# Planning GpSimd's instructions behind VectorE's shift passes, with a newly picked program order

## The chip, the core and the metric

The kernel runs on one core of a Trainium2 chip. The core's engines each execute their own instruction stream in order and meet only through semaphores: TensorE (PE; its weight loads are PEld), ScalarE (ACT), VectorE (DVE), GpSimd (POOL), and SyncE (SP), which here issues the DMAs. The metric is the device time of one execution in microseconds, lower is better. Time before: 1489.41 us, median of three runs (1488.92 to 1489.61).

## What is computed

Two rounds of attention block and feed-forward block on 2048 rows of width 512, with 32 heads of 16 columns:

```python
    x = A_x
    x = x + _A_ref(_layernorm(x, axis=-1), A_wqkv, A_wo)
    x = x + _B_ref(_layernorm(x, axis=-1), B_w1, B_b1, B_w2, B_b2)
    x = x + _A_ref(_layernorm(x, axis=-1), A_wqkv, A_wo)
    x = x + _B_ref(_layernorm(x, axis=-1), B_w1, B_b1, B_w2, B_b2)
    return x
```

`_A_ref` projects to q, k and v, computes `softmax(q k^T / 4) v` per head, and multiplies by `wo`. `_B_ref` is `gelu(x w1 + b1) w2 + b2` with 1792 hidden columns. Nearly all the work around the change is the exponential of the scores: 2 layers x 32 heads x 2048 x 2048 values.

## The kernel before, in words

**Cells.** The scores are cut into cells, each a PSUM bank of 128 keys by 512 columns (256 queries of two heads, or 512 queries of one, as the padded q tile `qp` has it). A layer has 2048 cells, the kernel 4096. A pass is one group of query columns and heads against all its key tiles. The score matmul of a cell (`score`, L1413) reads the keys and `qp`, which GpSimd makes by masking q (`qpad`, L1361).

**Two ways to the exponential.** ScalarE takes two or three cells in one ACTIVATE (`exps`, L1853) and writes bfloat16 into a `pt` buffer. Cells of five chosen key tiles (`KD`) may take the other way, here called D cells: VectorE evacuates one bank (`dfirst`, L1570) as a scaled and biased 16-bit integer, whose bits are a rough bfloat16 exponential; then three more copies of it, shifted by 32, 64 and 96 in the integer, are made, and TensorE adds the products of all four copies with V and three scaled copies of V (`vcopies`, L1342, on GpSimd). Two D cells share a buffer, a pair. For a pair (`dchain`) the first shift is made by GpSimd (L1687, 1024 columns); then VectorE makes both others in one instruction (L1692, 2048 columns), or GpSimd makes one of them (L1700) and VectorE the other (L1698, 1024 columns). L1692 and L1698 are "the shift passes of VectorE". In the program's names the pair buffers are `du`, and parts of `kt` and `v` that are free at the time serve as more of them.

**Who takes a cell.** A group of scores is issued for two or three banks. `swap` may turn the last cell of a group of three into a D cell when, in the planner's clocks, VectorE is free within SWAP us of the group's start; `attach` and `solo` can add D cells in other banks. So the share of the D cells is not fixed; it follows from how busy the planner believes VectorE to be.

**The order is written out by hand-made planning.** When the program is built, `_Sched` plays all work as threads against one clock per engine. `run` (L450) takes from each engine its best instruction that could go (those ready by the engine's clock by priority, else the one ready first), and of these commits the one with the earliest start, over and over. `_ready` (L379) gives the time at which an instruction could go; `_cost` its planned duration; `end` when its result is seen. What goes to the chip is only the order of each engine's instructions and the semaphore waits that data dependencies need. Planned times do not go to the chip.

**The shared port in the plan.** `_Op.port` marks VectorE's shift passes (and its writes of `OTT` and `NMR`). In the plan they never run at the same time as a GpSimd instruction. A marked instruction that would start while a committed GpSimd instruction runs is given that one's end, less HEAD (0.14 us), as ready time (`pool_ops`). A GpSimd instruction that would start while a committed marked one runs is moved behind it (`port_ops`): with a real semaphore wait (`op.lock`) if it would start within CLOSE (0.35 us) of the other's start, else only in the plan:

```python
            for a, b, ev in self.port_ops[-4:]:
                if a <= at < min(a + CLOSE, b - HEAD):
                    at = t = b + LATENCY["dve"]
                    op.lock = ev
                elif a <= at < b - HEAD:
                    at = t = b - HEAD
```

**Pieces.** The 4096 cells are cut into equal pieces of the program; `turn` sets the planner's constants for each piece to one of the ROWS (PIECES says which).

Of the kernel before, what the change touches and what calls it, by code (L numbers as in the profile page):

```python
# [34 lines left out]
DU = 10  # L35
LNP = 7
SWAP = 0.5
ALONE = 3.5
# [11 lines left out]
TAIL = 10  # L50
OPENING = 18
ROUNDS = 2
PTLOW = 5
TOL = 0.2
# [3 lines left out]
QUEUE = 4  # L58
LNQ = 3.5
NAMES = ("SWAP", "SLACK", "LATE", "TOL", "BACKLOG", "OPENING", "TAIL", "PVP", "PTURG", "DUURG", "DULOW", "DWIDE", "RWIDE", "PTLOW", "FPRIO", "MID",  # L60
         "EVAC", "ROUNDS", "ALONE", "AHEAD", "PSHIFT", "QUEUE", "SOLO", "BACK", "SIDE", "BOTH", "DMAX", "PMORE", "DUMORE",)
ROWS = (
# [239 lines left out]
class _Sched:  # L302
# [32 lines left out]
    def _advance(self, th):  # L335
        moved = False
        while th.op is None and not th.done:
# [37 lines left out]
            elif item[0] == "spawn":  # L375
                self.spawn(item[1], item[2])
        return moved

    def _ready(self, op):  # L379
        t = 0.0  # L380
        for k in op.reads:
# [1647 lines left out]
```

## Time and profile before

| | |
|---|---|
| median of the runs | 1489.41 us |
| the profiled execution | 1490.43 us, of which span 1488.6 us |
| ACT busy | 1457.6 us, 98% of the span |
| PE busy | 1432.6 us, 96% |
| DVE busy | 1353.7 us, 91% |
| POOL busy | 942.6 us, 63% |
| granted TensorE clock | 1.0 |

The span is from the first to the last instruction. "Busy" is the time in which an engine has an instruction running; an instruction that waits for something within the engine, after its semaphores, counts as busy for as long as it stands there. DVE's and ACT's neighbouring instructions overlap by some 0.08 us, so that counts times mean durations come out above the busy time.

### The profile page before, as it was taken

How to read it: one execution, taken by the hardware profiler on the slowest of the kernel's cores; microseconds unless marked ns; L12 is line 12 of the kernel's file. 1: busy time of each engine (PE TensorE's matmuls, PEld its weight loads, DVE VectorE, ACT ScalarE, POOL GpSimd, SP SyncE). 2: the span in 40 equal slices, each digit the busy share in tenths (PEclk: the TensorE clock that was granted, in tenths of full speed). 3: DMA queues.
4: the chain of work that ended last, by engine and by line, in shares of the span. 5: the costliest groups of instructions: out<-in, count | busy, mean ns of one | idle time of the engine just before them, and what ended most of it. 6: DMA issues, size and time to landing. Idle time of an engine off the chain costs nothing.

```text
span 1488.6 us, 46274 instructions
## 1 busy us (share of the span) xinstructions
PE 1432.6 (96%) x20012; PEld 436.7 (29%) x20012; DVE 1353.7 (91%) x2332; ACT 1457.6 (98%) x1387; POOL 942.6 (63%) x1032
## 2 busy tenths in 40 slices
PE   8999999999999999999999999999999999999999
PEld 2222222222222222222222222222222222334345
DVE  6589999999998999989879899999989999999994
ACT  7999999999999999999999999999999999999996
POOL 4347657676665776757556575667667667766751
PEclk9999999999999999999999999999999999999999
DMA  6100001153121430214421431001143104411021
GB/s 171 30 2 2 1 15 31 40 157 91 37 44 58 143 87 27 55 38 132 117 65 44 144 107 37 23 2 37 37 129 100 51 23 129 143 25 44 17 66 38
DMA packets 135798, 94.47 MB, mean 63 GB/s; under 512 B 36525, under 2 KB 134574, under 8 KB 135598
## 3 DMA queue, kind: packets, MB, share of 16 engines
q1 hardware_dynamic: 135598, 91.52, 22.1%
q8 instruction: 160, 2.62, 0.7%
q14 instruction: 40, 0.33, 0.1%
HBM read 79.70 MB, written 4.19 MB: 56 GB/s over the span
## 4 chain that ended last, share of the span: by engine, by line
ACT 49%; PE 37%; DVE 12%; POOL 1%; DMA 1%; issue 1%; SPq 0%
ACT pt L1853 42%; PE ps L653 12%; PE ps L1413 12%; PE ps L1917 12%; DVE du L1570 5%; ACT g L1128 3%; DVE du L1692 2%; DVE kt L1570 1%; ACT kt L1853 1%; ACT q L1853 1%; ACT L1128 1%; PE ps L1401 1%; DVE x L1167 1%; ACT L1853 1%; DVE g L1107 0%
## 5 line engine op out<-in xcount | busy, mean ns | idle before, releaser
L1853 ACT ACTIVATE pt<-ps 128x1024 bf16<-128x1024 f32 (+1 forms) x1253 | 1306.9, 1177 | 8.0 <-PE ps L1413 6.1
L1570 DVE TENSOR_SCALAR du<-ps 128x512 uint16<-128x512 f32 x853 | 564.9, 680 | 40.3 <-PE ps L1413 35.8
L1687 POOL TENSOR_SCALAR du<-du 128x1024 uint16<-128x1024 uint16 (+1 forms) x429 | 445.8, 1044 | 232.4 <-DVE du L1570 97.4
L1413 PE MATMUL ps<-qp,kt 32*128 32x512 bf16 x4096 | 548.4, 384 | 25.2 <-ACT pt L1853 13.6
L1917 PE MATMUL ps<-pt,v 128*17 128x512 bf16 (+1 forms) x3159 | 388.2, 359 | 3.4 <-ACT pt L1853 1.1
L1917 PE MATMUL ps<-du,vc 128*17 128x512 bf16 (+1 forms) x2874 | 346.9, 357 | 3.6 <-POOL v L1700 0.8
L1413 PEld LDWEIGHTS ps<-qp,kt 32*128 32x128 bf16 x4096 | 139.5, 91 | 576.5 <-ACT pt L1853 200.5
L1692 DVE TENSOR_SCALAR du<-du 128x2048 uint16<-128x2048 uint16 x336 | 245.4, 744 | 4.2 <-POOL du L1687 4.2
L1917 PE MATMUL ps<-du,v 128*17 128x512 bf16 (+1 forms) x958 | 158.6, 359 | 4.9 <-DVE xt L932 1.6
L1925 PE MATMUL ps<-b2row,zero 128*17 128x512 bf16 x788 | 145.5, 381 | 0.0
L653 PE MATMUL ps<-xf,wr 128*32 128x512 bf16 (+1 forms) x1888 | 128.5, 364 | 1.4 <-DVE g L1107 1.1
L1917 PEld LDWEIGHTS ps<-pt,v 128*17 128x17 bf16 x3159 | 95.6, 88 | 103.8 <-issue 70.4
L1361 POOL TENSOR_SCALAR qp<-q,mask 128x512 bf16<-128x512 bf16 (+1 forms) x91 | 61.4, 675 | 94.3 <-PE ps L1413 42.0
L1570 DVE TENSOR_SCALAR kt<-ps 128x512 uint16<-128x512 f32 x165 | 109.9, 681 | 10.5 <-PE ps L1413 9.7
L1917 PEld LDWEIGHTS ps<-du,vc 128*17 128x17 bf16 x2874 | 96.3, 89 | 76.2 <-issue 42.8
L1687 POOL TENSOR_SCALAR kt<-kt 128x1024 uint16<-128x1024 uint16 x83 | 86.9, 1048 | 49.3 <-DVE du L1692 23.1
L653 PE MATMUL ps<-wr,g 128*32 128x512 bf16 x1408 | 105.0, 383 | 1.1 <-DMA wr<-in_B_w_dram 0.5
L1342 POOL TENSOR_SCALAR vc<-v 128x680 bf16<-128x680 bf16 (+2 forms) x126 | 87.4, 693 | 25.4 <-DVE du L1692 8.2
L1700 POOL TENSOR_SCALAR du<-du 128x1024 uint16<-128x1024 uint16 (+1 forms) x93 | 97.1, 1044 | 8.4 <-DVE du L1692 4.4
L1917 PE MATMUL ps<-kt,vc 128*17 128x512 bf16 (+1 forms) x615 | 96.0, 339 | 1.2 <-DVE kt L1692 0.8
L1107 DVE TENSOR_SCALAR g<-ps,hb1t 128x512 bf16<-128x512 f32 (+1 forms) x112 | 79.0, 706 | 3.9 <-PE ps L653 3.6
L786 POOL TENSOR_SCALAR xln<-x,rstd,nmr 128x512 bf16<-128x512 bf16 x58 | 47.0, 818 | 21.9 <-DVE du L1692 10.9
(110 smaller groups left out, 1451.8 us busy)
## 6 DMA issues: line engine op xcount, KB each, us to landing
wr<-in_B_w_dram SPq DMA_DIRECT2D x228, 256.0 KB, 2.9
wr<-in_A_wqkv_dram SPq DMA_DIRECT2D x24, 256.0 KB, 2.9
x<-in_A_x_dram SPq DMA_DIRECT2D x7, 512.0 KB, 4.1
wr<-in_A_wo_dram SPq DMA_DIRECT2D x10, 256.0 KB, 3.3
kept<-x SPq DMA_DIRECT2D x4, 512.0 KB, 3.5
x<-kept SPq DMA_DIRECT2D x4, 512.0 KB, 3.9
out_dram<-x SPq DMA_DIRECT2D x16, 128.0 KB, 2.2
g<-in_A_wqkv_dram SPq DMA_DIRECT2D x3, 512.0 KB, 5.5
```

Of the source, the lines that this page charges most:

```text
L653: return [lambda e, a=a: e.matmul(out[32 * a:32 * a + 32, :], lhsT=lhsT[:, 32 * a:32 * a + 32], rhs=rhs, start=start, stop=stop, tile_posi ...
L1107: yield _Op("dve", 0.21 + n / 966, lambda e, fc=fc, pb=pb: e.tensor_scalar(T["G"][:, fc, q], pb, T["HB1T"][:, fc:fc + 1], None, op0=ALU.ad ...
L1342: yield _Op("pool", 0.15 + 0.133 * len(js), lambda e, i=i, w=w, v=v, js=js, src=src: e.tensor_scalar(T["VC"][:, v % 2, i, js[0]:js[-1] + 1 ...
L1361: yield _Op("pool", 0.27 + 0.42 * w / 512, lambda e, s=s, q=q, i=i, t=t, w=w: e.tensor_scalar(T["QP"][:, s, w * i:w * i + w], q, T["MASK"] ...
L1413: return (lambda e: e.matmul(o, lhsT=lhsT, rhs=rhs, start=True, stop=True, tile_position=(32 * a, 0)), ["K%d.%d.%d" % (l, gb, kt // 4), "Q ...
L1570: yield _Op("dve", 0.682, lambda e: e.tensor_scalar(u, self.bank(b), E_SCALE, E_BIAS, op0=ALU.mult, op1=ALU.add), reads=["B.%d" % b], writ ...
L1687: one = _Op("pool", 0.15 + 0.45 * n, lambda e, a=a, b=b: e.tensor_scalar(b, a, float(SHIFT), 1.0, op0=ALU.add, op1=ALU.mult), reads=key[0] ...
L1692: two = _Op("dve", 0.152 + 0.266 * n, lambda e: e.tensor_scalar(U[:, 2:4, 0:n, :], U[:, 0:2, 0:n, :], 2 * SHIFT, None, op0=ALU.add), reads ...
L1700: more = _Op("pool", 0.15 + 0.45 * n, lambda e, a=a, c=c: e.tensor_scalar(c, a, float(2 * SHIFT), 1.0, op0=ALU.add, op1=ALU.mult), reads=k ...
L1853: yield _Op("act", 0.065 + 0.4267 * n, lambda e, src=src, dst=dst: e.activation(out=dst, in_=src, func=ACT.Exp, scale=0.25), reads=["B.%d" ...
L1917: op.fns.append(lambda e, o=o, lhsT=q[0][0][m], rhs=q[0][1][:, n * m:n * m + n], a=a, st=st, sp=sp: e.matmul(o, lhsT=lhsT, rhs=rhs, start= ...
L1925: op.fns.append(lambda e, o=self.bank(b)[32 * a:32 * a + 17, :], rhs=rhs, a=a, st=not begun[a], sp=end: e.matmul(o, lhsT=T["ZERO"][:, 0:17 ...
```

## The change

Three things, all in the planner; no instruction's form is altered.

1. In `_ready`, a GpSimd instruction is now held, while a shift pass of VectorE (or another marked VectorE instruction) waits uncommitted whose data are there by GRACE = 1.5 us after the time at which the GpSimd instruction could start. Its ready time becomes that at which the marked one would end, less HEAD, if VectorE did it next. GALL = 1 makes this hold for all of GpSimd's instructions. A new function `bare` gives the data-ready time of the marked one.
2. The rows lose five constants (BACKLOG, OPENING, PTURG, DULOW, EVAC), which keep the values that they have in the module; there are 40 rows instead of 61.
3. PIECES has 80 entries instead of 160, each thus twice as long, with another choice.

```diff
+GRACE = 1.5
+GALL = 1
...
-NAMES = ("SWAP", "SLACK", "LATE", "TOL", "BACKLOG", "OPENING", "TAIL", "PVP", "PTURG", "DUURG", "DULOW", "DWIDE", "RWIDE", "PTLOW", "FPRIO", "MID",
-         "EVAC", "ROUNDS", "ALONE", "AHEAD", "PSHIFT", "QUEUE", "SOLO", "BACK", "SIDE", "BOTH", "DMAX", "PMORE", "DUMORE",)
+NAMES = ("SWAP", "SLACK", "LATE", "TOL", "TAIL", "PVP", "DUURG", "DWIDE", "RWIDE", "PTLOW", "FPRIO", "MID", "ROUNDS", "ALONE", "AHEAD", "PSHIFT",
+         "QUEUE", "SOLO", "BACK", "SIDE", "BOTH", "DMAX", "PMORE", "DUMORE",)
...
-PIECES = (10, 10, 15, 18, 18, 43, 56, 38, 30, 38, 38, 28, 8, 0, 60, 60, 48, 21, 43, 35, 46, 0, 1, 45, 45, 49, 4, 11, 41, 25, 57, 24, 20, 31, 15, 1,
...
+PIECES = (5, 10, 30, 21, 19, 33, 36, 8, 37, 23, 30, 38, 12, 0, 36, 22, 13, 0, 0, 0, 20, 35, 0, 0, 12, 0, 0, 18, 16, 0, 25, 33, 0, 17, 0, 0, 26, 3, 39,
...
+    def bare(self, op):
+        t = 0.0
+        for k in op.reads:
+            if k not in self.P.lastw:
+                return None
+        for ev in self.P.deps(op.reads, op.writes):
+            t = max(t, self.end.get(ev, 0.0) - OWN * (op.eng == "dve" == ev[0]))
+        return t
+
     def _ready(self, op):
...
         if op.eng == "pool":
             at, op.lock = max(t, self.clock["pool"]), None
+            if GRACE and (op.writes[0][:2] == "DU" or GALL):
+                for th in self.threads:
+                    x = th.op
+                    if x is not None and x.port and x.eng == "dve":
+                        y = self.bare(x)
+                        if y is not None and max(y, self.clock["dve"]) <= at + GRACE:
+                            t = max(t, max(y, self.clock["dve"], at) + self._cost(x) - HEAD)
+                at = max(t, self.clock["pool"])
             for a, b, ev in self.port_ops[-4:]:
                 if a <= at < min(a + CLOSE, b - HEAD):
                     at = t = b + LATENCY["dve"]
```

More of the change, by code (lines that the diff above doesn't have):

```diff
@@ L58 @@
 QUEUE = 4
+GRACE = 1.5
+GALL = 1
 LNQ = 3.5
-NAMES = ("SWAP", "SLACK", "LATE", "TOL", "BACKLOG", "OPENING", "TAIL", "PVP", "PTURG", "DUURG", "DULOW", "DWIDE", "RWIDE", "PTLOW", "FPRIO", "MID",
-         "EVAC", "ROUNDS", "ALONE", "AHEAD", "PSHIFT", "QUEUE", "SOLO", "BACK", "SIDE", "BOTH", "DMAX", "PMORE", "DUMORE",)
+NAMES = ("SWAP", "SLACK", "LATE", "TOL", "TAIL", "PVP", "DUURG", "DWIDE", "RWIDE", "PTLOW", "FPRIO", "MID", "ROUNDS", "ALONE", "AHEAD", "PSHIFT",
+         "QUEUE", "SOLO", "BACK", "SIDE", "BOTH", "DMAX", "PMORE", "DUMORE",)
 ROWS = (
[61 rows of a table removed]
-)
-PIECES = (10, 10, 15, 18, 18, 43, 56, 38, 30, 38, 38, 28, 8, 0, 60, 60, 48, 21, 43, 35, 46, 0, 1, 45, 45, 49, 4, 11, 41, 25, 57, 24, 20, 31, 15, 1,
[4 rows of a table removed]
[40 rows of a table added]
+)
+PIECES = (5, 10, 30, 21, 19, 33, 36, 8, 37, 23, 30, 38, 12, 0, 36, 22, 13, 0, 0, 0, 20, 35, 0, 0, 12, 0, 0, 18, 16, 0, 25, 33, 0, 17, 0, 0, 26, 3, 39,
+          4, 0, 3, 1, 19, 21, 13, 23, 0, 31, 28, 10, 7, 11, 6, 27, 2, 30, 34, 0, 15, 0, 27, 36, 32, 31, 29, 10, 33, 0, 16, 17, 14, 38, 24, 9, 19, 0,
+          0, 0, 0)
 CLOSE = 0.35
```

105 rows, old and new, of tables (PIECES, ROWS) are left out of this document.

## The prediction

> **What bounds the kernel now.** I read the page's busy times and chain first, then the middle of the execution as one stretch, then VectorE's shift passes one line at a time, then the waits.
>
> ```profile
> span 1488.6 us, 46274 instructions
> PE 1432.6 (96%) x20012; PEld 436.7 (29%) x20012; DVE 1353.7 (91%) x2332; ACT 1457.6 (98%) x1387; POOL 942.6 (63%) x1032
> ACT 49%; PE 37%; DVE 12%; POOL 1%; DMA 1%; issue 1%; SPq 0%
> ```
>
> The stretch from 50 to 1400 us (columns: length, then busy time and count of PE, PEld, DVE, ACT, POOL):
>
> ```profile
> 50.00:1400.00 1350.00, 1303.75 (x17640) 378.65 (x17640) 1258.15 (x2135) 1342.72 (x1264) 877.67 (x950) 1.00 0.22 61
> ```
>
> ScalarE works 1342.72 of 1350 us: 7.3 us of idle time in all. So in the middle the time is the work that ScalarE is given, and it changes only if (a) ScalarE gets other work, or (b) others keep it waiting. VectorE idles 91.9 us there, GpSimd 472. The groups of ScalarE's exponentials price (a):
>
> ```profile
> L1853 ACT ACTIVATE pt<-ps 128x1024 bf16<-128x1024 f32 x922 | 887.5, 1062 | 6.5 <-PE ps L1413 5.1
> L1853 ACT ACTIVATE pt<-ps 128x1536 bf16<-128x1536 f32 x330 | 472.7, 1499 | 1.4 <-PE ps L1413 1.0
> ```
>
> A group of three that loses a cell to VectorE costs 1499 - 1062 = 437 ns less. The price of a D cell, by VectorE's lines (min/median/max of one in ns) and groups:
>
> ```profile
> L1692 DVE TENSOR_SCALAR du<-du x336: 416/684/1668, 70.0 to 1459.6; 128x2048 uint16<-128x2048 uint16 x166, 128x1024 uint16<-128x1024 uint16 x2
> L1698 DVE TENSOR_SCALAR du<-du x93: 282/419/1304, 117.0 to 1461.1; 128x1024 uint16<-128x1024 uint16 x92, 128x512 uint16<-128x512 uint16 x1
> L1570 DVE TENSOR_SCALAR du<-ps 128x512 uint16<-128x512 f32 x853 | 564.9, 680 | 40.3 <-PE ps L1413 35.8
> L1692 DVE TENSOR_SCALAR du<-du 128x2048 uint16<-128x2048 uint16 x332 | 243.6, 748 | 4.2 <-POOL du L1687 4.2
> L1692 DVE TENSOR_SCALAR kt<-kt 128x2048 uint16<-128x2048 uint16 x58 | 41.0, 707 | 0.0
> L1692 DVE TENSOR_SCALAR v<-v 128x2048 uint16<-128x2048 uint16 x32 | 24.6, 777 | 2.0 <-POOL v L1687 1.9
> L1698 DVE TENSOR_SCALAR du<-du 128x1024 uint16<-128x1024 uint16 x92 | 47.3, 519 | 1.2 <-POOL du L1687 1.2
> L1698 DVE TENSOR_SCALAR kt<-kt 128x1024 uint16<-128x1024 uint16 x24 | 13.3, 556 | 0.0
> L1698 DVE TENSOR_SCALAR v<-v 128x1024 uint16<-128x1024 uint16 x7 | 3.9, 574 | 0.0
> ```
>
> A pair costs VectorE 2 x 680 + 684 = 2.04 us, a cell 1.02 us, if nothing disturbs the shift pass. The evacuations (L1570) are never disturbed (mean 680); the shift passes are: means above medians by 64, 23 and 93 ns (L1692) and 100, 137 and 155 ns (L1698), times their counts 21.2 + 1.3 + 3.0 + 9.2 + 3.3 + 1.1 = 39 us in all. The cause stands in this piece of the two timelines (start, duration):
>
> ```profile
> 704.18 1.04 POOL L1700 TENSOR_SCALAR du<-du 128x1024 uint16<-128x1024 uint16 x1
> 704.80 0.97 DVE L1692 TENSOR_SCALAR du<-du 128x2048 uint16<-128x2048 uint16 x1
> ```
>
> GpSimd's instruction had 0.42 us to go when the shift pass began, and that took 0.97 us instead of 0.68: it stood for 0.29 us, some 0.13 less than the rest of the other. The page "SBUF — State Buffer" of the Trainium skill (section "Who interferes with whom") says that the two engines share a port pair as an exclusive lock, that who issues first keeps it for the whole instruction, and that order, not shape, decides who blocks. The trace agrees up to the 0.13 us; what matters below is that by this rule too a GpSimd instruction that is let go first costs VectorE, whatever the plan believed.
>
> **The change, part by part.** *The hold itself.* It works on the moment at which the planner decides, and I followed one case through the code. Let a GpSimd instruction be able to go at `at`, and a shift pass be pending that VectorE will reach at a, later than `at`. Before, the GpSimd instruction has the earlier start, is committed, and the shift pass, which sees it, is planned behind it; VectorE's other work moves ahead. After, the GpSimd instruction is held, VectorE's evacuations and then the shift pass at a are committed; the shift pass cannot see what is not committed. Now nothing pending holds the GpSimd instruction any more, the hold is not kept, and its ready time is `at` again. The test for committed marked instructions asks a <= `at`, which is false. So it is planned at `at`, in front of the shift pass, with no wait written, and runs into it if a - `at` is below its length. On the chip it starts when its data are there, just as before. If on the other hand `at` lies at or after a, the shift pass had the earlier start anyway and both planners put GpSimd behind it, with the same real wait. These waits show before:
>
> ```profile
>   POOL du L1687: 117.3, 98
>   POOL qp L1361: 32.3, 19
> ```
>
> (GpSimd waiting for L1692 with du tiles: us, times.) So I expect the hold to write few new waits, and mostly to make VectorE's plan blind to GpSimd instructions that start ahead of a shift pass.
>
> *What blindness costs.* All shift passes: 332 + 58 + 32 + 92 + 24 + 7 = 545 in these rows. Below, it can cost nothing: the 39 us stay (a gain is rival A). Above, coordination is gone: the shift pass meets GpSimd at random. GpSimd is busy 877.67 / 1350 = 65% of the time, with instructions of mostly 1.05 us:
>
> ```profile
> L1687 POOL TENSOR_SCALAR du<-du 128x1024 uint16<-128x1024 uint16 x424 | 442.8, 1049 | 230.3 <-DVE du L1570 96.0 <-DVE du L1692 86.1 <-DVE kt L1692 20.9
> L1700 POOL TENSOR_SCALAR du<-du 128x1024 uint16<-128x1024 uint16 x92 | 96.5, 1049 | 7.1 <-DVE du L1692 3.1 <-DVE kt L1698 1.3 <-DVE du L1698 0.8
> L1700 POOL TENSOR_SCALAR kt<-kt 128x1024 uint16<-128x1024 uint16 x24 | 25.1, 1047 | 1.7 <-DVE du L1692 1.3 <-DVE du L1698 0.4
> L1700 POOL TENSOR_SCALAR v<-v 128x1024 uint16<-128x1024 uint16 x7 | 7.4, 1061 | 0.4 <-DVE du L1698 0.4
> ```
>
> The mean stand of a shift pass that meets one, less the 0.13 us, is (1.05 - 0.13)^2 / (2 x 1.05) = 0.40 us; 0.65 x 0.40 x 545 = 142 us. I take a point two thirds of the way, 39 + 0.67 x 103 = 108 us, because the blindness strikes what starts ahead of a pending shift pass and leaves what starts within one: +69 us on VectorE.
>
> *More L1700.* `dchain` gives GpSimd a second shift if its planned clock is at most about 1 us ahead of VectorE's. Under the hold GpSimd's decisions come late, VectorE's clock is then further on, and the test passes more often. Now 92 + 24 + 7 = 123 pairs have it; bounds are none more and all of the 332 + 58 + 32 = 422 others. I take half as many again, 62, near the present row: 62 x 1.05 = 65 us more on GpSimd, inside its 472 idle us, and 62 x (684 - 419) ns = 16 us less on VectorE.
>
> *The share of D cells.* `swap` looks at VectorE's planned clock; the 16 us pay for 16 / 1.02 = 16 more D cells, 16 x 0.437 = 7 us less on ScalarE. Bounds: none, and the 38 cells of rival A (below). A D cell also has four products with V on TensorE where the other has one:
>
> ```profile
> L1917 PE MATMUL ps<-du,vc 128*17 128x512 bf16 (+1 forms) x2874 | 346.9, 357 | 3.6 <-POOL v L1700 0.8
> ```
>
> 16 x 3 of these, four side by side, are 48 / 4 x 0.357 = 4 us, in the 1350 - 1303.75 = 46 us that PE idles; without that cover 4 us would be lost.
>
> *What covers it.* VectorE's balance is +69 - 16 + 16 = +69 us against 91.9 idle us. Not all of that is free: the part in which VectorE was ahead, waiting for the next score, is what a late VectorE eats first.
>
> ```profile
> DVE du L1570 <- PE ps L1413: 35.8, 111, 1.5
> DVE kt L1570 <- PE ps L1413: 9.7, 20, 3.1
> DVE v L1570 <- PE ps L1413: 5.0, 9, 1.6
> PEld ps L1413 <- DVE du L1570: 116.3, 275, 0.8
> ACT pt L1853 <- PE ps L1413: 6.1, 25, 0.5
> ```
>
> These are 50.5 us; 69 - 50.5 = 18.5 us come through. The way is the fourth and fifth row: the score matmuls already wait 116.3 us for an evacuation, behind them in PE's order stand the other scores, and ScalarE, which loses only 6.1 us to scores now, would lose the rest. Bounds: 0 (all cover) and 69 (none).
>
> *Rows and pieces.* The new choice changes the mix of orders with no new operation. From the trace it can be worth either sign; ScalarE's 7.3 idle us bound what order alone can win, and I put it at 0. Input DMAs, weight loads and SP's queue are not in a new place by rule, and the chain gives them 1%.
>
> **Sum.** Profiled execution 1490.43 (span 1488.6 and 1.8 around it) + 18.5 - 7 = 1501.9; the median of the runs stands 1.0 below that execution: 1501 us, 0.8% slower. Differences under 0.2% (3 us) are what a measurement of this kernel can't tell from none.
>
> **Rivals.** *A, faster: GpSimd is really kept off.* If the later commits make enough GpSimd instructions fall at or behind a, the 39 us of standing go, which is 39 / 1.02 = 38 D cells and 38 x 0.437 = 17 us of ScalarE: 1473 us. With the 62 pairs' relief it is another 7 us: 1466. For it: VectorE's priority lies with evacuations, so a shift pass is often reached directly after the evacuation that frees a GpSimd instruction, and then the real wait applies. Against it: those cases were planned so before. It decides if standing falls by over 5 us, with as many cells moved.
>
> *B, slower still: GpSimd becomes late in the order.* A pair then goes strictly in turn: GpSimd's shift 1.05, one evacuation ahead of the shift pass 0.68, the pass 0.68: 2.41 us. GpSimd's other work is 942.6 less the first shifts, 545 x 1.05 = 572, so 371 us; 1488.6 - 371 leaves room for 464 pairs, 81 fewer, 162 cells, 71 us of ScalarE. If half of it strikes: +35, 1524 us. For it: 63% and the passes' time nearly fill the port. Against: only the decision is late, not the start.
>
> *C, no change:* the decisions come later, the streams come out alike, and the new pieces give nothing: 1487 to 1492.
>
> Taken literally, the rule of the Trainium skill's page "SBUF — State Buffer" would have each meeting cost the full rest, 0.53 us on the mean instead of 0.40, and the upper end of the blindness would be 186 us; the trace shows the 0.13 us less, and its value is used.
>
> **Chances.** Main 0.42; A 0.35, because bare reordering by a new choice can also end there; B 0.14; C 0.09, of which 0.06 lies within 0.2%, 0.02 above it and 0.01 below. Faster 0.36, same 0.06, slower 0.58. Main's own range is 1492 to 1517 (10 us come through instead of 18.5; half of the 69 do). The whole range: 1468 leaves out A's far end, 1526 the upper half of B, together under 0.2.
>
> **What would show it.** Main: L1692's mean at some 870 ns (108 us over 545 passes) with its median still 684; the count of L1700 half as high again; ScalarE's idle time from 50 to 1400 us above 15; L1570 some 16 times more over all its tiles. A: L1692's mean under 720, L1570 up by over 35, fewer 128x1536 ACTIVATEs. B: L1570 down by over 70, and ScalarE still without idle time. My main step is wrong if the passes stand no longer than now: then only the choice of pieces is left.

## The result, and the profile after

The changed kernel takes 1575.09 us (median of 4 runs, 1572.9 to 1577.2) against 1489.16 us before: a ratio of 1.0569, 95% interval 1.0554 to 1.0583. That is 86 us more where 12 were forecast; the direction was right, the size far off, and the time lies outside the range given.

From the page of the changed kernel, the same three lines as of before:

```profile
span 1574.5 us, 45983 instructions
PE 1446.4 (92%) x19763; PEld 430.2 (27%) x19763; DVE 1454.7 (92%) x2404; ACT 1467.3 (93%) x1390; POOL 1084.9 (69%) x1119
DVE 71%; PE 22%; POOL 3%; ACT 3%; issue 1%; DMA 0%; SPq 0%
```

The chain that ended last was ScalarE's for 49% of the span; now it is VectorE's for 71% and ScalarE's for 3%. VectorE is busy 101.0 us longer than before (1454.7 - 1353.7), and the span grew by 85.9 us. ScalarE's idle time over the span rose from 31.0 to 107.2 us. Its idle time in the stretch from 50 to 1400 us (last of the five busy times but one) was 7.3 us and is now 75:

```profile
50.00:1400.00 1350.00, 1241.44 (x16003) 340.90 (x15995) 1274.06 (x2070) 1274.77 (x1195) 957.77 (x974) 0.99 0.21 60
```

VectorE's groups of the D cells in the changed kernel, by shape: count, busy us, mean ns of one, then the idle time of the engine just before them and what ended most of it. (L1566, L1688, L1694 are the lines that were L1570, L1692, L1698; L1683 and L1696 are GpSimd's L1687 and L1700; L1409 and L1849 are the scores' L1413 and ScalarE's L1853.)

```profile
L1566 DVE TENSOR_SCALAR du<-ps 128x512 uint16<-128x512 f32 x890 | 584.1, 677 | 28.5 <-PE ps L1409 26.8
L1688 DVE TENSOR_SCALAR du<-du 128x2048 uint16<-128x2048 uint16 x308 | 269.0, 879 | 3.8 <-POOL du L1683 3.4
L1566 DVE TENSOR_SCALAR kt<-ps 128x512 uint16<-128x512 f32 x173 | 115.2, 678 | 6.5 <-PE ps L1409 6.2
L1694 DVE TENSOR_SCALAR du<-du 128x1024 uint16<-128x1024 uint16 x133 | 84.8, 640 | 1.2 <-POOL du L1683 1.2
L1566 DVE TENSOR_SCALAR v<-ps 128x512 uint16<-128x512 f32 x80 | 53.2, 677 | 4.2 <-PE ps L1409 4.1
L1688 DVE TENSOR_SCALAR kt<-kt 128x2048 uint16<-128x2048 uint16 x49 | 44.0, 898 | 1.0 <-POOL kt L1683 1.0
L1694 DVE TENSOR_SCALAR kt<-kt 128x1024 uint16<-128x1024 uint16 x37 | 27.0, 730 | 0.0
L1688 DVE TENSOR_SCALAR v<-v 128x2048 uint16<-128x2048 uint16 x30 | 26.9, 899 | 1.3 <-POOL v L1683 1.3
L1694 DVE TENSOR_SCALAR v<-v 128x1024 uint16<-128x1024 uint16 x10 | 7.1, 708 | 0.0
```

and the two groups of the kernel before that the prediction did not show:

```profile
L1570 DVE TENSOR_SCALAR kt<-ps 128x512 uint16<-128x512 f32 x165 | 109.9, 681 | 10.5 <-PE ps L1413 9.7
L1570 DVE TENSOR_SCALAR v<-ps 128x512 uint16<-128x512 f32 x78 | 51.6, 678 | 5.2 <-PE ps L1413 5.0
```

Three readings. The D cells rose from 853 + 165 + 78 = 1096 to 890 + 173 + 80 = 1143, 47 more. The evacuations are as fast as ever (677 against 680 ns). The shift passes are not: above the undisturbed 684 and 419 ns stand 308 x 195 + 49 x 214 + 30 x 215 + 133 x 221 + 37 x 311 + 10 x 289 ns = 121 us, where it was 39. ("Standing" below is always this sum over the six groups.)

What a single stand looks like, from the timeline of VectorE and GpSimd in the changed kernel:

```profile
353.46 0.67 DVE L1566 TENSOR_SCALAR v<-ps 128x512 uint16<-128x512 f32 x1
354.06 0.68 DVE L1566 TENSOR_SCALAR du<-ps 128x512 uint16<-128x512 f32 x1
354.65 1.15 DVE L1688 TENSOR_SCALAR v<-v 128x2048 uint16<-128x2048 uint16 x1
354.22 1.04 POOL L1683 TENSOR_SCALAR v<-v 128x1024 uint16<-128x1024 uint16 x1 [0.96 <-DVE v L1566]
```

The evacuation that ended at 354.13 gave GpSimd its data, and GpSimd, idle for 0.96 us until then, started at 354.22. VectorE made one more evacuation and came to its pending shift pass at 354.65, 0.43 us behind GpSimd's start; the pass took 1.15 us. This has the shape of the case that the prediction followed through the code, with 354.22 for `at` and 354.65 for a. It is not a rare one: 275 shift passes of the changed kernel took over 0.06 us longer than undisturbed, and every one of them began while a GpSimd instruction was running.

The plans themselves, as the two kernels write them out when they are built, show how this came about. In the plan of before, 22 of 551 shift passes start with over 0.15 us of a GpSimd instruction still to go; in the changed plan it is 358 of 576, and in all 358 the GpSimd instruction was committed after the pass. The real waits written for the port fall from 284 to 180. By its own clocks the changed plan ends at 1455 us, 20 us before that of the kernel before: the planner took it for the faster one.

And the waits of the changed kernel (us in total, times, longest):

```profile
PEld ps L1409 <- DVE du L1566: 224.1, 442, 1.5
PEld ps L1409 <- ACT pt L1849: 122.3, 258, 2.0
ACT pt L1849 <- PE ps L1409: 66.7, 161, 1.6
```

The score matmuls wait 224.1 us for VectorE's evacuations (116.3 before) and less for ScalarE (122.3 us, 200.5 before), and ScalarE waits 66.7 us for scores (6.1 before): the way that the prediction named, with eleven times the wait at its end.

### The profile page after: what moved, and what is told of

Same layout as the page of the kernel before. It is cut to its first block, busy times and chain, and to the rows that moved or that the text cites. A ratio compares the mean times of both kernels' runs of the same rounds, so it can differ in the third digit from the quotient of the medians.

```text
span 1574.5 us, 45983 instructions
## 1 busy us (share of the span) xinstructions
PE 1446.4 (92%) x19763; PEld 430.2 (27%) x19763; DVE 1454.7 (92%) x2404; ACT 1467.3 (93%) x1390; POOL 1084.9 (69%) x1119
## 4 chain that ended last, share of the span: by engine, by line
DVE 71%; PE 22%; POOL 3%; ACT 3%; issue 1%; DMA 0%; SPq 0%
DVE du L1566 27%; DVE du L1688 13%; PE ps L649 8%; PE ps L1409 7%; PE ps L1913 6%; DVE kt L1566 5%; DVE du L1694 4%; DVE g L1103 4%; DVE v L1566 3%; DVE kt L1688 2%; ACT pt L1849 2%; DVE v L1688 1%; DVE stats L756 1%; DVE kt L1694 1%; DVE xt L928 1%; DVE x L986 1%
## 5 line engine op out<-in xcount | busy, mean ns | idle before, releaser
L1849 ACT ACTIVATE pt<-ps 128x1024 bf16<-128x1024 f32 (+1 forms) x1157 | 1215.8, 1140 | 72.7 <-PE ps L1409 66.7
L1683 POOL TENSOR_SCALAR du<-du 128x1024 uint16<-128x1024 uint16 (+1 forms) x449 | 483.4, 1082 | 235.1 <-DVE du L1566 140.5
L1409 PE MATMUL ps<-qp,kt 32*128 32x512 bf16 x4096 | 552.2, 386 | 67.0 <-DVE du L1566 38.0
L1566 DVE TENSOR_SCALAR du<-ps 128x512 uint16<-128x512 f32 x890 | 584.1, 677 | 28.5 <-PE ps L1409 26.8
L1913 PE MATMUL ps<-pt,v 128*17 128x512 bf16 (+1 forms) x2881 | 375.5, 361 | 5.8 <-DVE du L1688 2.3
L1913 PE MATMUL ps<-du,vc 128*17 128x512 bf16 (+1 forms) x3003 | 362.7, 361 | 11.1 <-DVE du L1688 8.7
L1409 PEld LDWEIGHTS ps<-qp,kt 32*128 32x128 bf16 x4096 | 139.7, 91 | 634.1 <-DVE du L1566 224.1
L1688 DVE TENSOR_SCALAR du<-du 128x2048 uint16<-128x2048 uint16 (+1 forms) x311 | 270.7, 876 | 3.8 <-POOL du L1683 3.4
L1696 POOL TENSOR_SCALAR du<-du 128x1024 uint16<-128x1024 uint16 (+1 forms) x138 | 154.8, 1121 | 2.9 <-DVE du L1688 2.3
L1566 DVE TENSOR_SCALAR kt<-ps 128x512 uint16<-128x512 f32 x173 | 115.2, 678 | 6.5 <-PE ps L1409 6.2
L1683 POOL TENSOR_SCALAR kt<-kt 128x1024 uint16<-128x1024 uint16 x87 | 95.5, 1098 | 32.6 <-DVE kt L1566 14.0
L1357 POOL TENSOR_SCALAR qp<-q,mask 128x512 bf16<-128x512 bf16 (+1 forms) x91 | 71.2, 783 | 63.9 <-PE ps L1409 41.6
L1921 PE MATMUL ps<-b2row,zero 128*17 128x512 bf16 x547 | 111.6, 383 | 0.0
L1913 PE MATMUL ps<-kt,vc 128*17 128x512 bf16 (+1 forms) x645 | 105.1, 339 | 4.3 <-DVE kt L1688 2.3
L1694 DVE TENSOR_SCALAR du<-du 128x1024 uint16<-128x1024 uint16 (+1 forms) x138 | 87.6, 636 | 1.2 <-POOL du L1683 1.2
```

Source lines behind the costliest of these rows:

```text
L1409: return (lambda e: e.matmul(o, lhsT=lhsT, rhs=rhs, start=True, stop=True, tile_position=(32 * a, 0)), ["K%d.%d.%d" % (l, gb, kt // 4), "Q ...
L1566: yield _Op("dve", 0.682, lambda e: e.tensor_scalar(u, self.bank(b), E_SCALE, E_BIAS, op0=ALU.mult, op1=ALU.add), reads=["B.%d" % b], writ ...
L1683: one = _Op("pool", 0.15 + 0.45 * n, lambda e, a=a, b=b: e.tensor_scalar(b, a, float(SHIFT), 1.0, op0=ALU.add, op1=ALU.mult), reads=key[0] ...
L1688: two = _Op("dve", 0.152 + 0.266 * n, lambda e: e.tensor_scalar(U[:, 2:4, 0:n, :], U[:, 0:2, 0:n, :], 2 * SHIFT, None, op0=ALU.add), reads ...
L1694: far = _Op("dve", 0.151 + 0.134 * n, lambda e: e.tensor_scalar(U[:, 3, 0:n, :], U[:, 1, 0:n, :], 2 * SHIFT, None, op0=ALU.add), reads=key ...
L1696: more = _Op("pool", 0.15 + 0.45 * n, lambda e, a=a, c=c: e.tensor_scalar(c, a, float(2 * SHIFT), 1.0, op0=ALU.add, op1=ALU.mult), reads=k ...
```

## The experiments

### Which half of the change costs

First: the hold alone, on the rows and pieces of before; the rows and pieces alone (GRACE = 0); and blindness without any hold.

The hold alone, in the kernel before (with `bare`, as the change has it):

```diff
+GRACE = 1.5
+GALL = 1
...
+            if GRACE and (op.writes[0][:2] == "DU" or GALL):
...
+                            t = max(t, max(y, self.clock["dve"], at) + self._cost(x) - HEAD)
```

> The kernel before with the hold (GRACE 1.5, GALL 1) added, its own 61 rows and 160 pieces kept. Theory 'blind' (the hold makes VectorE's plan blind to GpSimd instructions that start ahead of a shift pass; the passes stand for them and VectorE becomes the bound): 1540 to 1600 us, the shift passes standing for over 100 us in all (39 before), ScalarE idle for over 60 us. Rival 'pieces' (the new rows and pieces are what costs): 1489 us, within 10.

Measured 1583.94 us, ratio 1.0635 (1.0592 to 1.0678), standing 115 us. One group of it:

```profile
L1711 DVE TENSOR_SCALAR du<-du 128x2048 uint16<-128x2048 uint16 x284 | 241.9, 860 | 9.0 <-POOL du L1706 8.6
```

The rows and pieces alone, in the changed kernel:

```diff
-GRACE = 1.5
+GRACE = 0
```

> The changed kernel with GRACE 0: the new rows and 80 pieces without the hold. Theory 'blind': 1485 to 1510 us, the shift passes standing for 30 to 60 us, ScalarE busy to within 20 us of the middle stretch. Rival 'pieces': 1560 us or more.

Measured 1503.14 us, ratio 1.0092 (1.0063 to 1.0122), standing 45 us. The same group:

```profile
L1688 DVE TENSOR_SCALAR du<-du 128x2048 uint16<-128x2048 uint16 x308 | 227.2, 755 | 9.2 <-POOL du L1683 9.1
```

So the hold makes the loss. The new rows and pieces cost 14 us where there is no hold (29 D cells fewer than before, 1067, and ScalarE busy 11.7 us longer), and with it they are 9 us better than the old ones (1575 against 1584). That a choice of pieces goes with the planner's rules under which it was picked is the likely reason; no run separates it.

Blindness without the hold, in the kernel before:

```diff
-            for a, b in self.pool_ops[-6:]:
+            for a, b in []:
                 if a < at + HEAD and at < b - HEAD:
                     at = t = b - HEAD
```

> The kernel before, without any hold, whose planner no longer moves a shift pass behind a committed GpSimd instruction (the test of pool_ops is emptied; the data's waits stay). This is blindness by itself, without any late decision for GpSimd. Theory 'blind': 1540 to 1600 us, over 100 us of standing. Rival 'late' (what costs is that GpSimd's instructions are decided late and the order of their consumers suffers): under 1510 us.

Measured 1597.58 us, ratio 1.0726 (1.0695 to 1.0758), standing 133 us. One group of it:

```profile
L1692 DVE TENSOR_SCALAR du<-du 128x2048 uint16<-128x2048 uint16 x314 | 274.7, 885 | 10.9 <-POOL du L1687 10.7
```

A planner that simply does not look at GpSimd when it places a shift pass gives the same picture as the hold: 885 ns against 879 for the pass, and a loss of the same kind, a little larger. Nothing in this kernel decides GpSimd's instructions later, so blindness is enough to make a loss of this size.

### Taking the stands away by real waits

The changed kernel with its order untouched, but with a real wait wherever a GpSimd instruction was planned into a shift pass that begins after it:

```diff
             if e == "pool" and op.lock:
                 self.P.wait(e, *op.lock)
+            if e == "pool":
+                for a, b, late in self.port_ops[-6:]:
+                    if start < a < start + self._cost(op) - HEAD:
+                        self.P.wait(e, *late)
```

> The changed kernel with the same planned order on every engine, but a GpSimd instruction that was planned to start ahead of an already committed shift pass and to run into it gets a real wait on that pass. Theory 'blind': standing falls under 40 us and the time to 1500 to 1545 us, since VectorE gets back some 80 us and GpSimd has over 400 us of idle time to pay with. Rival 'late': standing falls too, but the time stays above 1560 us, because GpSimd's results come later still.

Measured 1596.21 us, ratio 1.0717 (1.0686 to 1.0748). Its busy times, its shift pass, and who keeps GpSimd (L1687, L1692 here are L1683, L1688 of the changed kernel):

```profile
PE 1453.8 (91%) x19763; PEld 430.5 (27%) x19763; DVE 1421.0 (89%) x2404; ACT 1465.1 (92%) x1390; POOL 1047.8 (66%) x1119
L1692 DVE TENSOR_SCALAR du<-du 128x2048 uint16<-128x2048 uint16 x308 | 239.2, 782 | 31.2 <-POOL du L1687 30.6
```

```profile
POOL du L1687 <- DVE du L1692: 125.7, 113, 3.0
```

This missed. Standing fell only to 88 us, VectorE's busy time by 34 us, and the span grew by 20 us over the changed kernel (1594.2). By the row shown GpSimd now waits 125.7 us for shift passes (44.6 in the changed kernel, 86.7 before). Neither theory had this right. The waits do not keep GpSimd from the other passes that come by: some 28 us of the standing are on GpSimd instructions that had just waited for another shift pass, some 56 us on ones that follow directly on another instruction of GpSimd's. And they make the pairs later: VectorE's shift passes now wait 51 us in all buffers for GpSimd's shifts (30.6 of it in the group shown), where it was 7 us in the changed kernel. So VectorE stands 33 us less and waits 44 us more. It left open whether the stands alone make up the 86 us; the last pair of runs below bears on that.

### How much of an unplanned delay comes through

The prediction let 50.5 of VectorE's 91.9 idle us cover stands. To price this by itself, the kernel before got unplanned work: a small instruction in front of shift passes, which the planner does not count, so that the order stays that of before.

```diff
+        extra = [lambda e, i=i: e.bn_stats(T["SCR"][:, i, :], T["IDENT"][:, 0:96]) for i in range(1)]
...
+            if self.shifts % 1 == 0:
+                op.fns = extra + [own]
```

That is the spread form; the lumped one has `0:128`, `range(4)` and `% 5`, the half dose `% 2`.

> The kernel before, its plan unchanged, with one small VectorE instruction (statistics of 96 columns, into a tile that nothing reads) put ahead of every shift pass, of which the planner knows nothing: 551 unplanned delays of an estimated 0.15 us each, some 83 us, as much as the change added in standing. Theory 'through' (unplanned time on VectorE reaches the end almost one for one, whatever VectorE's idle time): 1555 to 1590 us. Rival 'cover' (VectorE's 132 idle us take half or more of it; long single stands are what hurts): under 1530 us.

> The same with four instructions of 128 columns ahead of every fifth shift pass: 110 unplanned delays of an estimated 0.75 us, some 83 us, single ones as long as the stands on the port. Theory 'through': 1555 to 1590 us, within 10 us of the spread form. Rival 'long ones hurt': 20 us or more above the spread form.

> The spread form with the small instruction ahead of every second shift pass only: half the dose, some 43 us more VectorE time than the kernel before. Theory 'in proportion' (each unplanned us on VectorE costs the end a fixed share, 0.79 by the spread form and 0.78 by the lumped one): span 1488.6 + 0.79 x 43 = 1522 us, within 6. Rival 'idle time covers first' (the prediction's step: some 50 us of VectorE's idle time are eaten before anything comes through): under 1500 us.

Measured 1559.43 us (ratio 1.0464, 1.0424 to 1.0505) spread, 1547.15 us (1.0382, 1.0352 to 1.0412) lumped, 1509.48 us (1.0136, 1.0116 to 1.0156) at half the dose. The spans and busy times of the profiled executions, one fence each, in the order half, lumped, spread:

```profile
span 1508.8 us, 46618 instructions
PE 1441.9 (96%) x20012; PEld 436.5 (29%) x20012; DVE 1387.0 (92%) x2607; ACT 1464.9 (97%) x1387; POOL 939.0 (62%) x1032
```

```profile
span 1545.2 us, 46714 instructions
PE 1446.3 (94%) x20012; PEld 434.4 (28%) x20012; DVE 1426.1 (92%) x2772; ACT 1474.0 (95%) x1387; POOL 943.0 (61%) x1032
```

```profile
span 1555.8 us, 47123 instructions
PE 1449.3 (93%) x20012; PEld 432.9 (28%) x20012; DVE 1439.2 (93%) x2883; ACT 1477.6 (95%) x1387; POOL 939.7 (60%) x1032
```

| | VectorE busy, more than before | span, more than before | difference | VectorE idle in the span | of this, evacuations waiting for scores |
|---|---|---|---|---|---|
| before | 0 | 0 | 0 | 134.9 | 50.5 |
| half | 33.3 | 20.2 | 13.1 | 121.8 | 39.6 |
| lumped | 72.4 | 56.6 | 15.8 | 119.1 | 38.6 |
| spread | 85.5 | 67.2 | 18.3 | 116.6 | 32.3 |
| the change | 101.0 | 85.9 | 15.1 | 119.8 | 37.1 |

All in us; the last row is the changed kernel itself, which lies close to the line that the three doses draw. Each adds 13 to 18 us less to the span than to VectorE. So some 15 us are covered and the rest passes nearly one for one; some 120 us of VectorE's idle time were of no use in any of the four. The last column shows where the cover comes from: the 50.5 us that the prediction meant to spend shrink by 11 to 18 us and no further. Of the two ideas in the last expectation neither held as put: "in proportion" by 0.79 gives 26 us at the half dose (measured 20.2), and the cover that comes first exists, but with 15 us, not 50. Spread or lumped makes little difference beyond the dose; the lumped form fell 8 us short of its range, with a dose of 72.4 us where 83 were estimated.

The line is that of an unchanged plan under delays. Where the plan is another, the span can grow by more than VectorE's work: the hold alone adds 86.2 us to VectorE and 91.1 to the span (1579.7), blindness alone 103.3 and 107.7 (1596.3). So it is in part luck that the change, whose plan differs too, lies so near the line; but nowhere did anything like 50 us disappear.

### Giving the planner a truer price, or a truer hold

```diff
-            return max(op.cost - OVERLAP, 0.07)
+            return max(op.cost - OVERLAP, 0.07) + 0.22 * (op.port and op.writes[0][:2] == "DU")
```

> The changed kernel, whose planner counts 0.22 us more for each shift pass (the mean stand that the trace shows), hold and pieces as they are. If the loss comes from VectorE being given more than it can do (too many D cells, a plan too early throughout): fewer D cells than 1143, and 1510 to 1545 us. If it comes from each single unforeseen stand: 1560 us or more.

Measured 1546.18 us, ratio 1.0375 (1.0345 to 1.0406). D cells fell to 1075 and standing only to 102 us: a planner that knows the mean gives VectorE less to do, and gets 29 us back of the 86; the stands remain. The time is 1 us above the range of the first idea, so that one is the nearer, though not the whole.

The hold made good keeps the GpSimd instruction behind the shift pass once that is committed:

```diff
+            if op.behind:
+                t = max(t, op.behind[0] + LATENCY["dve"])
+                at, op.lock = max(t, self.clock["pool"]), op.behind[1]
...
                 self.port_ops.append((start, start + cost, ev))
+                for x in self.threads:
+                    if x.op is not None and x.op.held:
+                        x.op.behind = (start + cost, ev)
```

> The changed kernel with the hold made good: a GpSimd instruction that was held for a shift pass stays planned behind it once that is committed, and gets a real wait on it. Theory 'late GpSimd' (GpSimd cannot be kept off without starving the pairs): standing under 30 us, D cells down by over 40 from 1143, 1500 to 1560 us. Rival 'the idea was right, only not carried out': standing under 30 us and 1480 us or less.

Measured 1525.75 us, ratio 1.0238 (1.0209 to 1.0268). Groups of this kernel:

```profile
L1697 DVE TENSOR_SCALAR du<-du 128x2048 uint16<-128x2048 uint16 x347 | 236.3, 683 | 39.1 <-POOL du L1692 38.0
L1575 DVE TENSOR_SCALAR du<-ps 128x512 uint16<-128x512 f32 x784 | 522.2, 683 | 76.7 <-PE ps L1418 72.9
L1575 DVE TENSOR_SCALAR kt<-ps 128x512 uint16<-128x512 f32 x154 | 103.7, 683 | 13.7 <-PE ps L1418 13.2
L1575 DVE TENSOR_SCALAR v<-ps 128x512 uint16<-128x512 f32 x70 | 47.0, 682 | 5.7 <-PE ps L1418 5.4
L1858 ACT ACTIVATE pt<-ps 128x1536 bf16<-128x1536 f32 x363 | 518.9, 1499 | 1.0 <-PE ps L1418 0.4
L1692 POOL TENSOR_SCALAR du<-du 128x1024 uint16<-128x1024 uint16 x393 | 408.7, 1043 | 317.8 <-DVE du L1697 188.3 <-DVE kt L1697 59.8 <-DVE du L1575 21.9
```

The pass takes its undisturbed 683 ns, standing is 4 us in all, and yet the kernel is slower than before. Nothing was added but what keeps the held instruction behind the pass, so the changed kernel's stands came from the hold being dropped. Now it is the prediction's rival B that one sees: GpSimd idles 317.8 us in front of this one group, 248.1 of it for shift passes (188.3 + 59.8; before, 107.0 of 230.3); D cells fall to 784 + 154 + 70 = 1008, 88 fewer than before, and 88 x 0.437 = 38 us of ScalarE's work answer to the 35.4 us by which the span grew (1524.0). The idea carried out costs less than half of what the change costs, but it costs: 36 us against the kernel before, 23 us against the same rows and pieces without a hold. Rows and pieces picked for a real hold were not tried.

A short hold, made good as above, with the rows and pieces of before:

```diff
-GRACE = 1.5
+GRACE = 0.3
```

> The kernel before, rows and pieces its own, with the hold made good (as in the fourth run of the second study) but with GRACE 0.3 instead of 1.5 us: GpSimd gives way only to a shift pass that VectorE reaches within 0.3 us. If the idea pays where GpSimd gives away little: standing under 20 us, D cells not under 1096, 1475 to 1488 us. If giving way costs pairs at any length: fewer D cells and 1495 us or more.

Measured 1503.15 us, ratio 1.0095 (1.0078 to 1.0112); D cells 1083, standing 34 us. Giving way for a short time buys little standing and still loses cells.

More real waits in the kernel before:

```diff
+            if e == "pool":
+                for a, b, late in self.port_ops[-6:]:
+                    if a <= start < b + 0.3:
+                        self.P.wait(e, *late)
```

> The kernel before, order and planned times unchanged; a GpSimd instruction that is planned within a committed marked VectorE instruction or up to 0.3 us after it gets a real wait on it, where until now it had one only if it was moved behind it within 0.35 us of its start. If part of the 39 us of standing comes from GpSimd running ahead of its plan: standing under 30 us and 1480 to 1488 us. If it does not: standing unchanged and 1489 us or a little more for the waits.

Measured 1491.45 us, ratio 1.0018 (1.0008 to 1.0028), with standing no smaller (42 us; the pass of du at 757 ns, 748 before). So the 39 us are not GpSimd running up to 0.3 us ahead of its plan. None of these versions beats the kernel before.

### The stands alone

GpSimd's shifts made short, in the changed kernel and in that of before, with everything else in the planned order:

```diff
-            one = _Op("pool", 0.15 + 0.45 * n, lambda e, a=a, b=b: e.tensor_scalar(b, a, float(SHIFT), 1.0, op0=ALU.add, op1=ALU.mult),
+            one = _Op("pool", 0.15 + 0.45 * n, lambda e, a=a, b=b, m=m: e.tensor_scalar(b[:, 0:m], a[:, 0:m], float(SHIFT), 1.0, op0=ALU.add, op1=ALU.mult),
```

(`m` is 32, or all columns in three of the buffers; the second shift of GpSimd alike. Both kernels leave out the other columns of these copies, so they price the order and are of no other use.)

> The changed kernel with its whole planned order, but GpSimd's shifts (the first of a pair, and the second where it makes one) work on 32 columns of 1024 in all pair buffers but three; the other columns are left as they are, so that part of the shifted copies is not computed. Five early loads fill the pair buffers' other rows first. GpSimd hardly holds the port then, while VectorE's and TensorE's instructions stay what they were. Theory 'stands' (the 86 us are the stands on the port alone): shift passes standing under 40 us and a span of 1465 to 1495 us, ScalarE bound again. Rival 'order' (later decisions, more D cells and the new order cost by themselves): 1520 us or more.

> The control: the kernel before with the same shortened GpSimd shifts and early loads. Both theories: 1475 to 1492 us, ScalarE bound as before; what it differs from 1489 by is the price of the means (loads, earlier results), to be taken off the other run.

Measured 1476.3 us for the changed kernel's order (ratio 0.9907, 0.9878 to 0.9936) and 1485.95 us for the control (0.9972, 0.9961 to 0.9984). The changed kernel's order with short GpSimd shifts:

```profile
span 1474.3 us, 45993 instructions
PE 1419.9 (96%) x19763; PEld 429.7 (29%) x19763; DVE 1340.6 (91%) x2404; ACT 1439.9 (98%) x1390; POOL 510.8 (35%) x1119
L1692 DVE TENSOR_SCALAR du<-du 128x2048 uint16<-128x2048 uint16 (+1 forms) x311 | 218.4, 708 | 0.3 <-POOL du L1687 0.3
```

and its control:

```profile
span 1484.0 us, 46284 instructions
PE 1431.1 (96%) x20012; PEld 437.7 (29%) x20012; DVE 1321.0 (89%) x2332; ACT 1455.1 (98%) x1387; POOL 452.0 (30%) x1032
```

Standing is 15 us, VectorE 114 us less busy, ScalarE again busy for 98% of the span, and the span 100 us below that of the changed kernel, of which the control, 4.6 us below before, gives the price of the means. On the same footing the changed kernel's order is 10 us faster than that of before: its 47 more D cells relieve ScalarE (1439.9 against 1455.1 us busy), as they were planned to. So the order costs nothing by itself. Short shifts also bring GpSimd's results earlier, so this pair alone does not part the stands from late results of GpSimd. But late results are hardly there in the changed kernel: by the groups shown, its shift passes wait 3.4 + 1.2 + 1.0 + 1.3 = 6.9 us for GpSimd. That leaves the stands.

## Why the prediction was right in direction and wrong in size

**The mechanism held.** The hold makes VectorE's plan blind: for 358 of 576 passes GpSimd's instruction is put in front of the pass only after the pass itself has its place. The hold alone (1584 us) and blindness alone (1598 us) both give the loss, a hold that is kept takes the stands away (4 us), and the trace has cases of the shape that was worked out. That few new waits would be written came out too: there are even fewer (180, 284 before). The rule of the Trainium skill's page "SBUF — State Buffer" ("Who interferes with whom": who issues first keeps the port) agrees up to 0.14 us: GpSimd's start at 354.22 cost the pass at 354.65 some 0.47 us, 0.14 less than the 0.61 us that GpSimd had to go.

**Terms that came out.** Standing: 108 us forecast, 121 measured, between my point and the upper end of 142. The pass's mean: 870 ns forecast, 879 measured. More L1700: 62 forecast, and 186 in place of 124 counted over all sizes, 62 more; but the 62 was picked between 0 and 422 with no row to fix it, so the exact hit is luck. The reason given for it, late decisions, is not all of it either: the blind kernel without a hold has 166.

**The share of D cells was mis-sized.** I let the 16 us of relief alone pay for more cells: 16. It is 47, most likely because the planner, not seeing the stands, also believes VectorE free more often: the blind kernel without a hold has 34 more than before, and the changed kernel with 0.22 us counted for each pass has 68 fewer than without. At 1.02 us that is 48 us of VectorE instead of 16. The sum for VectorE, +69 us, should have been 82 of standing - 16 + 48 = +114; the busy time shows +101, as neighbouring instructions overlap 15 us more than before, which the sum does not price. The relief of ScalarE, priced at 7 us, would have been 20, but is worth nothing once ScalarE is not the bound. Rows and pieces, put at 0, are no 0 either: 14 us without the hold, 9 us the other way with it.

**The step that failed is the cover.** "These are 50.5 us; 69 - 50.5 = 18.5 us come through." The runs with known doses show 13 to 18 us of cover, and in the changed kernel the three rows behind the 50.5 us still hold 26.8 + 6.2 + 4.1 = 37.1 us. VectorE's idle time while it waits for scores was not a reserve: what is late there makes the next scores late (224.1 us of waiting of the score matmuls), so the wait moves on with the delay. With 13 to 18 in place of 50.5 and +101 in place of +69 the same step gives 83 to 88 us; measured is 85.9. Of the 67 us between the forecast 18.5 and this, 32 are the load and some 35 the cover; with only one of the two put right the step would give 50 to 56 us. My upper bound for this step was 69, all of it through; with the right load that bound would have held the result.

**The rivals.** A did not occur: standing rose. Its other half, that the idea would pay if carried out, did not come true in the two real holds that were tried (1526 and 1503 us). B did not occur in the change: D cells rose and the passes hardly wait for GpSimd; it did, with the cells and the price of its kind, when the hold was made good. C is out.

**What stays open.** The run with real waits at an unchanged order is 20 us slower than the change, with 33 us less standing. VectorE's 44 us more of waiting for GpSimd's shifts outweigh that; whether the rest is the lower clock (0.986 against 0.994, see below) or the order, no run separates. Why the kernel before has 39 us of standing, where by its plan it would be 9, was not found; more waits did not lower it.

## What to carry to other kernels

In a planner that commits by earliest start, holding an instruction back changes who is seen when a competitor is placed; if the hold is not turned into a time or a wait, the held instruction still runs first, and the plan no longer knows. Idle time on an engine that is tied in a loop to the bound one (evacuation, bank, score, evacuation) need not be cover; here 13 to 18 of 135 us were. Test it with a known unplanned dose, and count what exceeds the small part that disappears as coming through whole. A change that frees time in the plan also changes how much work the plan hands out, so the load has to be priced along with the delay.

## What the runs showed of the hardware that I had not expected

The stand on the port is very regular: in the 275 passes of the changed kernel that stood, it is what GpSimd's instruction still had to go by its recorded span, less 0.137 to 0.140 us in eight of ten of them. It is the 0.13 us that the prediction took from one pair.

TensorE's clock was not always granted in full in the kernels with much standing: 0.994 over the profiled execution of the changed kernel, 0.986 with the real waits, against 1.000 before. Both kernels from 140 to 200 us, the changed one first:

```profile
140.00:200.00 60.00, 54.15 (x577) 12.82 (x573) 52.85 (x83) 51.51 (x44) 44.45 (x45) 0.89 0.00 1
```

```profile
140.00:200.00 60.00, 55.87 (x690) 14.93 (x686) 58.01 (x94) 59.78 (x52) 39.88 (x43) 1.00 0.01 2
```

TensorE is busy 54.15 us of 60 and yet has a clock of 0.89: fewer matmuls (577 against 690), hardly more idle time by the busy figure, went with the lower clock; which of the two came first the trace does not say. Its part in the 86 us is small: the run of the changed kernel at 0.999 took 1572.9 us, the profiled one at 0.994 took 1576.3 us.
